# Windows 4 and 5 in 64-token chunks, and one written list for the steady part of a fused attention and MLP kernel

## The chip, the cores and the metric

The kernel runs on one core of a Trainium2 chip. The metric is the device time of one execution in microseconds, as the median of several runs; the profile is one execution that the hardware profiler recorded. PE is TensorE (PEld its weight loads), DVE is VectorE, ACT is ScalarE, POOL is GpSimd, SP is SyncE, which here issues DMAs.

## What is computed

A linear attention with a decay per head, and an MLP behind it with a residual. The reference, cut:

```python
# q, k, v: batch 4, heads 8, tokens 768, head size 64; lam: one decay per head; block = 64
for b in range(nb):
    intra = einsum('bhic,bhjc->bhij', qb, kb) * Dmask        # lam ** (i - j) below the diagonal
    intra = einsum('bhij,bhjd->bhid', intra, vb)
    inter = einsum('bhid,bhde->bhie', qb * lam_pow, kv_state)
    out[:, :, sl] = intra + inter
    kv_state = lam_block * kv_state + einsum('bhsd,bhse->bhde', kb * rev_pow, vb)
# x = out as (4, 768, 512); w_ch1 is 512 x 2048, w_ch2 is 2048 x 512
xn = (x - mu) / sqrt(var + 1e-06) * g_ln
result = x + maximum(xn @ w_ch1, 0) @ w_ch2
```

The length of a chunk is free: with longer chunks the product inside a chunk grows and the states are fewer.

## The kernel before

The work is cut into 12 windows of 256 tokens, u = 0 to 11; window u is of batch u % 4 and holds two pairs (ab = 0, 1) of 64-token blocks. Windows up to 5 (LB = 6) work in chunks of 128 tokens, the others in chunks of 64. A window goes through these steps:

- load_in (L93) issues the DMAs of k, q and v on SP's queue. fill (L72) takes one DMA per tensor for u < LB, whose rows hold two tokens (512 bytes), and two DMAs in rows of one token (256 bytes) otherwise.
- in_k_one, in_q_one and in_v (L229, L233, L239) cast to bf16 and multiply by the decays, mostly on POOL; transpose_dma (L254) transposes q and k by DMA on SP's queue, for windows up to 2 transpose_pe (L244) does it on TensorE.
- With 128 tokens: kv (L311) makes k'v on TensorE; scores and mask (L266, L285) make the masked scores in two halves of the heads; new_state (L337) adds the old state on VectorE and decays the sum on POOL. av (L427) multiplies the masked scores by v into the PSUM tiles po0 and po1.
- With 64 tokens: kv64, scores64, mask64 (L379, L361, L374) and av64 (L416, 32 matmuls where av has 64). states64 (L393) makes, for each j = 0, 1, a sum over the old state (Smid, L405), a second sum (Stmp, L408), the decayed state on POOL (L410) and a copy on POOL (L413). The sums of j = 1 need the decayed state of j = 0.
- inter (L441) adds q times state; norm (L462) copies x to SBUF on ScalarE with its sum, and centers it on VectorE (xc, L477). to_xT (L494) transposes xc: on TensorE for u = 2, 3, 4 (X_PE), else by DMA. rstd_of (L513) makes the squares and the reciprocal root on ScalarE and VectorE.
- The MLP of a window (mlp, L532) is cut into units: m1 (L539, or m1_tile, L651) of 8 or 16 matmuls and a ReLU on ScalarE; then m2 (L667) for windows up to 3, with finish (L700, L708) on VectorE, or m2w (L644) for the later ones. w_sums (L802) makes sums of w2 on VectorE, and h_sums (L557) sums of the hidden units.

[...] kv(u, "po") writes into po0 and po1, which av of the same window writes again; a new tile waits until all who use the old one are done.

The order is written out by hand. The statement manual_schedule() makes every engine issue its instructions in the order in which the program's statements stand, so that an engine's queue is the list of statements, cut to those of this engine. The steady part (L1041 to L1361) takes the units of the MLP from one plan: units(n) issues the next n of it, and between them stand the steps of the windows. For windows 3, 4 and 5 the step is s12(u) (L886: kv, scores, masks, states), then two to four units, then s3(u) (L899: av, inter), one unit or two, and s4(u) (L909). Window 5's last part and window 6 share X1 and X2 (L938, L945); from window 7 on X(u) (L953) holds the second half of window u-1 and the first half of window u.

## Time and profile before

| what | value |
|---|---|
| median of 3 runs | 208.19 us |
| lowest, highest | 207.92, 208.30 us |
| span of the profiled execution, first to last instruction | 205.7 us |
| PE, DVE, ACT, POOL busy | 195.9, 133.4, 122.0, 83.9 us |
| matmuls, and DMA packets under 512 bytes | 3223, 65121 |

For the profiled execution its span is what is told; the runs' times are whole executions, with what lies ahead of the first and behind the last instruction. A row of a timeline gives the start in us from the span's beginning, the length in us, the engine, the line, the operation, out<-in with sizes, how many instructions were merged, and in brackets the idle time before it with what ended it. In the chain of waits a row is a start, a length, the engine, tile and line, and the number of instructions. In the groups, busy us and the mean ns of one stand behind the first bar.

### The profile page before, as it was taken

The page shows a single profiled execution, that of the slowest core. Times are in us where ns is not written, and L with a number is a line of the kernel's source. Part 1 is how long each engine was busy: PE and PEld are TensorE (multiplying, and loading weights), DVE is VectorE, ACT ScalarE, POOL GpSimd, SP SyncE. Part 2 cuts the span into 40 slices and gives each one's busy share as a digit, 9 for nine tenths or more (in the row PEclk, how much of TensorE's full clock was granted, in tenths as well). Part 3 has the DMA queues.
Part 4 walks back from the last instruction along what each step waited for, and adds up shares of the span by engine and source line. Part 5 has one row for each costly group of instructions (what it writes and reads, how often), then busy time and mean ns, then how long its engine had stood idle before and what let it go on. Part 6 is the DMA issues. An engine that isn't in the chain of part 4 may idle for free.

```text
span 205.7 us, 7488 instructions
## 1 busy us (share of the span) xinstructions
PE 195.9 (95%) x3223; PEld 157.8 (77%) x3223; DVE 133.4 (65%) x277; ACT 122.0 (59%) x281; POOL 83.9 (41%) x117
## 2 busy tenths in 40 slices
PE   1997999999999999999999999999999999999992
PEld 0485798545784686489889888888888888988881
DVE  3588352626766458777889774857877947865253
ACT  3787678535357468166575775585586565652630
POOL 5557039317656341464273261772273202002020
PEclk9999999999999999999999999999999999999999
DMA  3999999999899998999799999887988020178404
GB/s 105 301 255 203 179 281 192 198 293 277 194 268 252 217 183 190 170 256 213 165 201 134 220 213 135 207 169 128 234 133 183 4 51 3 26 131 273 139 7 97
DMA packets 91011, 36.41 MB, mean 177 GB/s; under 512 B 65121, under 2 KB 88161, under 8 KB 90978
## 3 DMA queue, kind: packets, MB, share of 16 engines
q1 hardware_dynamic: 86368, 31.53, 74.9%
q0 software_dynamic: 4224, 4.19, 12.7%
q8 instruction: 25, 0.41, 0.9%
q10 hardware_dynamic: 386, 0.20, 0.4%
q14 instruction: 8, 0.07, 0.1%
HBM read 27.27 MB, written 6.29 MB: 163 GB/s over the span
## 4 chain that ended last, share of the span: by engine, by line
PE 85%; DMA 6%; DVE 2%; ACT 2%; SPq 1%; issue 1%; POOL 0%; POOLq 0%; DVEq 0%
PE pm L547 34%; PE pm L684 14%; PE pm1t L658 6%; PE pwd L582 6%; PE pwa L582 6%; PE pwc L582 6%; DMA w<-in_moe_w_ch_dram 4%; PE pwb L582 3%; DMA qin<-in_q_dram 3%; PE po L449 2%; PE po L436 2%; DVE x L595 1%; PE po L423 1%; PE sc L370 1%; PE sc L279 1%; PE pk L324 1%
## 5 line engine op out<-in xcount | busy, mean ns | idle before, releaser
L547 PE MATMUL pm<-xT,w 128*128 128x256 bf16 x640 | 73.9, 273 | 0.4 <-DMA w<-in_moe_w_ch_dram 0.4
L547 PEld LDWEIGHTS <-w 128*128 128x128 bf16 x640 | 61.2, 98 | 8.7 <-DMA w<-in_moe_w_ch_dram 0.5
L550 ACT ACTIVATE hT<-pm 128x512 f16<-128x512 f32 x80 | 47.1, 597 | 28.7 <-PE pm L547 28.5
L684 PE MATMUL pm<-w,hT 128*128 128x512 f16 x128 | 29.8, 380 | 0.0
L582 PEld LDWEIGHTS <-hs 128*128 128x128 f16 x256 | 24.9, 98 | 2.9
L607 POOL TENSOR_TENSOR x<-ev_u,x 128x256 f32<-128x256 f32 x8 | 5.9, 743 | 48.8 <-ACT ev_u L606 37.4
L330 POOL TENSOR_TENSOR Sn<-Stmp,lam_s 128x256 bf16<-128x256 f32 x16 | 9.8, 616 | 33.0 <-DVE Stmp L408 17.9
L565 DVE TENSOR_TENSOR hs<-hT 128x1024 f16<-128x1024 f16 x16 | 12.7, 795 | 15.8 <-ACT hT L550 14.5
L684 PEld LDWEIGHTS <-hT 128*128 128x128 f16 x128 | 11.8, 98 | 12.4
L582 PEld LDWEIGHTS <-hT 128*128 128x128 f16 x192 | 18.7, 98 | 2.1
L658 PE MATMUL pm1t<-xT,w 128*128 128x128 bf16 x256 | 15.6, 219 | 1.0 <-DMA w<-in_moe_w_ch_dram 0.7
L477 DVE SCALAR_TENSOR_TENSOR xc<-po,nmean,g_row 128x512 bf16<-128x512 f32 x18 | 13.0, 745 | 5.0 <-ACT nmean L476 4.9
L658 PEld LDWEIGHTS <-w 128*128 128x128 bf16 x256 | 14.8, 98 | 1.5 <-DMA w<-in_moe_w_ch_dram 0.8
L475 ACT ACTIVATE x<-po 128x512 f32<-128x512 f32 x18 | 10.6, 590 | 7.8 <-PE po L449 4.5
L242 POOL TENSOR_TENSOR vb<-vin,lam_v 128x1024 bf16<-128x1024 f32 (+1 forms) x7 | 11.6, 1659 | 4.8 <-DMA vin<-in_v_dram 4.7
L520 ACT ACTIVATE sq<-x,nmean 128x512 bf16<-128x512 f32 x18 | 12.9, 719 | 0.3
L242 POOL TENSOR_TENSOR vb<-vin,lam_p 128x1024 bf16<-128x1024 f32 x6 | 11.4, 1896 | 3.1 <-ACT hT L550 1.9
L289 DVE TENSOR_TENSOR mA<-sc,keep 128x512 bf16<-128x512 f32 x14 | 9.0, 682 | 4.9 <-PE sc L279 4.9
L661 ACT ACTIVATE hT<-pm1t 128x512 f16<-128x512 f32 x16 | 9.6, 598 | 4.4 <-PE pm1t L658 4.3
L595 DVE SCALAR_TENSOR_TENSOR x<-pwd,rstd,x 128x256 f32<-128x256 f32 x16 | 7.7, 481 | 3.4 <-POOL x L615 3.4
L595 DVE SCALAR_TENSOR_TENSOR x<-pwa,rstd,x 128x512 f32<-128x512 f32 (+1 forms) x16 | 9.1, 612 | 0.8
L582 PE MATMUL pwa<-w,hT 128*128 128x256 f16 x64 | 9.6, 273 | 0.0
(137 smaller groups left out, 318.0 us busy)
## 6 DMA issues: line engine op xcount, KB each, us to landing
out_dram<-x SPq DMA_DIRECT2D x22, 256.0 KB, 4.0
w<-in_moe_w_ch_dram POOLq DMA_DIRECT2D x8, 512.0 KB, 8.0
kin<-in_k_dram SPq DMA_DIRECT2D x14, 256.0 KB, 5.2
qin<-in_q_dram SPq DMA_DIRECT2D x14, 256.0 KB, 4.2
vin<-in_v_dram SPq DMA_DIRECT2D x14, 256.0 KB, 5.3
kin<-in_k_dram SPq DMA_DIRECT2D x5, 512.0 KB, 6.2
qin<-in_q_dram SPq DMA_DIRECT2D x5, 512.0 KB, 7.0
vin<-in_v_dram SPq DMA_DIRECT2D x5, 512.0 KB, 6.1
```

What stands on the lines that cost most here:

```text
L242: eng.tensor_tensor(st[u]["vb"][:, hs], qkv_in[u]["v"][:, hs], lv.to_broadcast([128, n, 2, D]), op=ALU.mult)
L330: eng.tensor_tensor(dst, src, lam_s[:, :, None].to_broadcast([128, NP, D]), op=ALU.mult)
L475: nc.scalar.activation(x, po, ACT.Copy, accum_out=sm)
L477: nc.vector.scalar_tensor_tensor(xc, in0=po, scalar=nm, in1=g_row, op0=ALU.add, op1=ALU.mult)
L520: nc.scalar.activation(sq, s["x"][:, ab], ACT.Square, bias=s["nmean"][:, ab:ab + 1], accum_out=ss[:, ab:ab + 1])
L547: nc.tensor.matmul(pm[:, b, :], lhsT=w1[n // W2K][:, kk, (n % W2K) * 128:(n % W2K + 1) * 128], rhs=xT_of[g][:, kk, 0:N], start=(b == 0 and ...
L550: nc.scalar.activation(hT[:, u * NB:(u + 1) * NB, 0:N], pm, ACT.Relu)
L565: nc.vector.tensor_tensor(s13, b[:, :, 1:2, :].to_broadcast([128, n, 2, 128]), b[:, :, 0:4:3, :], op=ALU.subtract)
L582: nc.tensor.matmul(pr[bank], lhsT=lhs(r), rhs=rhs, start=(first and r == 0), stop=(r == KB // 2 - 1), skip_group_check=True)
L595: nc.vector.scalar_tensor_tensor(out, in0=in0, scalar=r[ab], in1=in1, op0=ALU.mult, op1=ALU.add)
L658: nc.tensor.matmul(pm[:, b, :], lhsT=w1[c][:, kk, b * 128:(b + 1) * 128], rhs=xT_of[g][:, kk, i * 128:(i + 1) * 128], start=(b == 0 and kk ...
L684: nc.tensor.matmul(acc[i], lhsT=hT[:, kk, i * 128:(i + 1) * 128], rhs=w2[kk // W2K][:, kk % W2K, :], start=(kk == 0), stop=(kk == KB - 1))
```

## The change

LB goes from 6 to 4, so windows 4 and 5 are loaded, scaled and multiplied in the form with 64 tokens. kv64 gets a tag for its PSUM tiles. states64 is cut into sums64 (VectorE) and pools64 (POOL), norm's centering becomes center, the squares leave rstd_of as squares, and wind_up of the last window is cut into wind_up and wind_down. Steps such as s12, s3, X are gone: the steady part is one list of single statements, in which each unit of the MLP is named (m1g[g](n), m2s[g](i, part), m2s[g].w(n)). The units keep their order except for a few of windows 0 and 1, for m1g[7](7) and m2s[7].w(0), which change places, and for the first of window 11, which goes ahead of three units. Most steps stand between the same units as before. The core of the diff:

```diff
-    LB = 6
+    LB = 4
...
-    def kv64(u):
+    def kv64(u, tag="mm"):
...
-        s["pk"] = [mm_tile([128, 2, NP, D], F32, f"pk{ab}") for ab in range(2)]
+        s["pk"] = [ps.tile([128, 2, NP, D], F32, tag=f"po{ab}" if tag == "po" else tag, bufs=dict(mm=4, sc=2, po=1)[tag],
+                           name=f"pk{ab}") for ab in range(2)]
...
-    def states64(u, j):
+    def sums64(u, j):
...
+    def pools64(u, j):
...
+    def center(u, ab):
+        s = st[u]
+        po = s["po"][ab].rearrange("p h d -> p (h d)")
+        nc.vector.scalar_tensor_tensor(s["xc"][:, ab], in0=po, scalar=s["nmean"][:, ab:ab + 1], in1=g_row,
+                                       op0=ALU.add, op1=ALU.mult)
...
-    transpose_pe(2, 0, (0, 1, 2, 3), nc.vector)
-    units(1)
-    transpose_pe(2, 1, (0, 1, 2, 3))
+    transpose_pe(2, 1, (0, 1, 2, 3))
     transpose_pe(2, 0, (0, 1, 2, 3), nc.vector)
+    m1b(4)
...
     load_in(3, "k", nc.sync)
+    load_in(3, "v", nc.sync)
     load_in(3, "q", nc.sync)
...
     in_q_one(4, nc.gpsimd, 0)
     in_q_one(4, nc.gpsimd, 1)
-    transpose_dma(4, 0)
     transpose_dma(4, 1)
     load_in(5, "v", nc.sync)
+    in_k_one(4, nc.gpsimd, 1)
...
+    m1g[2](0)
+    transpose_dma(4, 0)
+    m1g[2](1)
+    w_sums(0, 1)
+    m1g[2](2)
+    m1g[2](3)
+    scores(3, 0, early=True)
+    kv(3, "po")
+    new_state(3, 0, nc.gpsimd)
+    scores(3, 1)
+    mask(3, 0)
+    w_sums(1, 0)
     in_v(4, nc.gpsimd)
+    mask(3, 1)
+    new_state(3, 1, nc.gpsimd)
+    m1g[2](4)
+    m1g[2](5)
+    m1g[2](6)
...
+    m1g[2](7)
+    av(3, range(NP))
+    inter(3, 0, fence=False)
+    reader(3)
+    norm(3, 0)
+    m2s[2](0, 0)
+    inter(3, 1)
+    norm(3, 1)
+    center(3, 1)
...
+    m2s[2](0, 3)
+    m2s[2](1, 0)
     transpose_dma(5, 0)
+    center(3, 0)
     to_xT(3, 0)
     to_xT(3, 1)
...
-    units(2)
-    s12(4)
+    m2s[2](1, 1)
+    m2s[2](1, 2)
+    kv64(4, "po")
+    scores64(4)
+    sums64(4, 0)
+    pools64(4, 0)
+    mask64(4, 0)
+    sums64(4, 1)
+    pools64(4, 1)
+    mask64(4, 1)
+    av64(4)
     open_window(6)
+    open_window(7)
     in_k_one(6, nc.scalar, 0)
-    in_k_one(6, nc.gpsimd, 1)
-    units(2)
-    open_window(7)
-    units(2)
-    s3(4)
-    units(1)
+    m2s[2](1, 3)
+    m1g[3](0)
+    m1g[3](1)
+    m1g[3](2)
+    inter(4, 0, fence=False)
+    reader(4)
+    m1g[3](3)
...
-    s12(5)
+    m2s[3](0, 0)
+    m2s[3](0, 1)
+    m2s[3](0, 2)
+    kv64(5, "po")
+    scores64(5)
+    sums64(5, 0)
+    pools64(5, 0)
+    mask64(5, 0)
+    sums64(5, 1)
+    pools64(5, 1)
+    mask64(5, 1)
+    av64(5)
     transpose_dma(6, 1)
-    units(1)
+    m2s[3](0, 3)
```

## The prediction

> **What bounds the kernel now.** I began with the busy time by engine and by stage, because it says whether any engine has idle time that a better order could use.

> ```profile
> 79.00:92.00 13.00, 13.00 (x293) 8.29 (x292) 10.12 (x24) 6.36 (x17) 5.11 (x8) 1.00 1.17 198
> ...
> sum 205.70, PE 195.90 PEld 157.84 DVE 133.44 ACT 122.04 POOL 83.86; mean PE 9.79 PEld 7.89 DVE 6.67 ACT 6.10 POOL 4.19
> ```

> The columns after the stretch are its length and then the busy time of PE, PEld, DVE, ACT and POOL, the granted clock, the DMA share and GB/s. In the 13 us in which windows 5 and 6 are worked on, PE is busy for all 13.00. Over the whole span it is busy for 195.90 of 205.70 us, and what is missing lies in the first 21 us and after the last MLP units. So in the part that the change rewrites TensorE is the bound, without holes. Two things follow: an edit there can gain only as much matmul time as it takes away, and every microsecond for which an edit makes TensorE wait is added to the end in full, since no later hole takes it up.

> Next I read the chain of waits around window 4, because it gives TensorE's order and the real length of each piece.

> ```profile
> 68.88 0.38 PE pk L324 x32
> 69.25 0.23 PE sce L279 x16
> 69.48 0.22 PE sc L279 x16
> 69.70 0.97 PE pm L684 x4
> 70.67 2.62 PE pm L547 x24
> 73.29 0.64 PE po L436 x64
> ```

> This is exactly the order in which the statements stand: kv(4), both halves of the scores, four units of the MLP, then av(4). The four units (0.97 + 2.62 = 3.59 us) are the cover under which VectorE masks the scores and sums the states. TensorE takes its instructions as they are listed, and av(4) does not wait, since its masks are finished when the units are.

> **The change, part by part.**

> *Matmuls of windows 4 and 5.* The form with 64 tokens is run already for windows 6 to 11, so its pieces have rows.

> ```profile
> 88.00 0.29 PE pk L389 x32
> ...
> 101.42 0.37 PE po L423 x32
> ...
> 102.43 0.28 PE sc L370 x32
> ```

> Before, a window takes 0.38 + 0.23 + 0.22 + 0.64 = 1.47 us for these products; in the new form it takes 0.29 + 0.28 + 0.37 = 0.94. If nothing waited, that would be 0.53 us less for each window, 1.06 for both. inter keeps its matmuls.

> *Where av64 now stands.* The new list has kv64(4), scores64(4), the sums, the state products on POOL and the masks, and then av64(4), with m2s[2](1, 3) only behind it; for window 5 it is the same, with m2s[3](0, 3) behind. Between the scores and av64 TensorE has nothing of the MLP. av64 multiplies by the masked scores, and it writes the PSUM tiles po0 and po1, in which kv64(u, "po") has just left the sums that VectorE still reads. So it waits for VectorE's whole chain. Window 7 shows that chain in the same order (sums of j=0, mask, sums of j=1), and window 6 shows how soon it starts after the products:

> ```profile
> 102.47 0.42 DVE L405 TENSOR_TENSOR Smid<-pk,Sn 128x256 f32<-128x256 f32 x1
> 103.00 0.43 DVE L408 TENSOR_TENSOR Stmp<-pk,Smid 128x256 f32<-128x256 f32 x1
> 103.35 0.68 DVE L376 TENSOR_TENSOR mA<-sc,keep 128x512 bf16<-128x512 f32 x1
> 104.16 0.42 DVE L405 TENSOR_TENSOR Smid<-pk,Sn 128x256 f32<-128x256 f32 x1
> 104.61 0.42 DVE L408 TENSOR_TENSOR Stmp<-pk,Smid 128x256 f32<-128x256 f32 x1
> ```
> ```profile
> 88.37 0.42 DVE L405 TENSOR_TENSOR Smid<-pk,Sn 128x256 f32<-128x256 f32 x1 [0.36 <-PE pk L389]
> ```

> The products of window 6 end at 88.00 + 0.29 = 88.29 and the first sum starts at 88.37, 0.08 later. From the first sum to the end of the last one it is 104.61 + 0.42 - 102.47 = 2.56 us, and the second mask behind it takes 0.68 more, 3.24, or a little less where two instructions overlap; I take 3.2. Only the first four matmuls of av64 (pair 0, even head) can go ahead of the second mask. From the start of kv64 to the end of av64 it is 0.29 + 0.08 + 3.2 + 0.37 = 3.94 us in which TensorE does nothing else, where 1.47 us of matmuls stood before: 2.47 us more for a window, 4.9 for both. The scores run inside the wait, and behind the waiting av64 the whole MLP is queued. From below, 2.3 us a window: the first sums could start when the first half of the products is there, about half of 0.29 earlier. From above, 3.0: VectorE may still be at the weight sums or at q of window 6 when window 5's products end, or its instructions may be slowed.

> *center(3, 0).* It moves from behind norm(3, 0) to a place behind m2s[2](1, 0), right ahead of the transposes that read it. On VectorE that puts it behind the reciprocal of rstd_of(3) and the last step of m2s[2](0, 3).

> ```profile
> 64.14 0.75 DVE L477 SCALAR_TENSOR_TENSOR xc<-po,nmean,g_row 128x512 bf16<-128x512 f32 x1 [0.58 <-ACT nmean L476]
> 64.81 0.41 DVE L811 TENSOR_TENSOR wt<-w,wt 128x512 f16<-128x512 f16 x1
> 65.26 0.42 DVE L812 TENSOR_TENSOR wt<-wt,w 128x512 f16<-128x512 f16 x1
> 66.02 0.17 DVE L525 RECIPROCAL rstd<-std 128x2 f32<-128x2 f32 x1 [0.34 <-ACT std L521]
> 66.10 0.73 DVE L708 SCALAR_TENSOR_TENSOR x<-pm,rstd,x 128x512 f32<-128x512 f32 x1
> ```
> ```profile
> 66.70 0.45 PE xt L510 x8
> ```

> The last step (L708) ends at 66.83 and a centering takes 0.75, so xc is there at 67.58, where TensorE comes to the transposes at 66.70: 0.9 us of waiting. Nothing hides it, since the units around it stand where they stood. The lower end is 0.

> *The sums of w2 inside window 3.* w_sums(1, 0) moves from ahead of the window's products to a place between its masks, and new_state(3, 1), whose reading of po1 av(3) waits for, comes behind it.

> ```profile
> 60.12 0.41 DVE L334 TENSOR_TENSOR Stmp<-pk,Sn 128x256 f32<-128x256 f32 x1
> ```
> ```profile
> 61.17 0.64 PE po L436 x64
> ```

> That sum ends at 60.53, so av(3) at 61.17 has 0.64 us in hand; two more weight sums (0.41 + 0.42, as in the rows above) use 0.83. I take 0.2 us of waiting, between 0 and 0.9 (in case they run at half speed beside POOL).

> *The transposes of window 2.* q's transposes now stand ahead of k's, and one half of q comes from POOL:

> ```profile
> 30.79 1.55 POOL L236 TENSOR_TENSOR kq<-qin,lam_q 128x512 bf16<-128x512 f32 x1 [0.34 <-DMA qin<-in_q_dram]
> ```
> ```profile
> 32.19 0.45 PE tp L250 x8
> ```

> POOL ends at 32.34 and TensorE comes at 32.19: 0.2 us, between 0 and 0.3.

> *Loads and queues.* With LB = 4 the loads of windows 4 and 5 run as twelve DMAs of 256 KB in rows of 256 bytes where six of 512 KB in rows of 512 bytes stood, and k of window 4 is transposed behind q and behind the loads of v of window 5, on SP's queue; q of window 3 is loaded behind its v.

> ```profile
> kin<-in_k_dram SPq DMA_DIRECT2D x14, 256.0 KB, 5.2
> ...
> kin<-in_k_dram SPq DMA_DIRECT2D x5, 512.0 KB, 6.2
> ```
> ```profile
> 55.53 5.16 SPq L257 DMA_TRANSPOSE kqT<-kq  x2
> ```
> ```profile
> DMA to landing us min/median/max: 3.3/4.4/7.7
> ```

> Two halves that land 5.2 us after their issue cost between nothing more than one 6.2 us load (they overlap) and 2 x 5.2 - 6.2 = 4.2 us more (one after the other). I take nothing on the path: the transposes of window 4 are all issued by 55.53 + 5.16 = 60.69, and the scores that read them came at 69.25, 8.6 us later, against a median of 4.4 to landing. That cover is thinner in the new order; what it costs when gone is a rival below. POOL gets two state copies more per window and in_v(3), in_v(4) later; the next that need POOL are the states of window 4, after all of that by the same rows. [...]

> *The rest of the list* (squares, readers, masks in another order, stores, wind_down in two, m1g[11](0) two units earlier) changes the order on engines that wait for TensorE, or swaps TensorE's work with TensorE's work: nothing, give or take 0.3 us. The work behind the last units is the same.

> **The sum.** 4.9 + 0.9 + 0.2 + 0.2 = 6.2 us. The profiled span of 205.7 us becomes 211.9. The median of the runs is 208.19 (207.92 to 208.3), 2.5 us above that span for what lies around it; I leave that as it is: 208.2 + 6.2 = **214.4 us**.

> **The rivals.**

> *The wait isn't there* (the other side). If TensorE reached av64 with the masks done, only the smaller products would be left: 208.2 - 1.06 = 207.1 us, faster. It decides from the point at which the 3.2 us chain is covered: some 3 us of units would have to run between scores64 and av64, so that order on TensorE would have to differ from the list. For it: nothing in the profile. Against it: the chain of waits shows the listed order around kv(4) and av(4) to the unit. 4 in 100. This is also the case in which the change doesn't do what it says.

> *The transposes of window 4 come late.* If the added pieces and the new place on SP's queue delay k's transposes by 4.2 us and the landing is the slow one (7.7), they land at 60.69 + 4.2 + 7.7 = 72.6, where scores64(4) would come at about 69.2 + 1.3 = 70.5 (the small waits ahead of it). Up to 2 us more: 214.4 to 216.4. For it: DMA share 1.17 in the stage, a full queue. Against it: medians. 16 in 100.

> *The clock falls in the waits.* TensorE's matmuls were slow at the start of the span:

> ```profile
> 6.55 0.63 PE L752 MATMUL idle<-keep_h,ident 128*128 128x512 bf16 x1
> ```
> ```profile
> L684 PE MATMUL pm<-w,hT 128*128 128x512 f16 x128 | 29.8, 380 | 0.0
> ```

> A matmul over 512 columns takes 0.63 us there and 0.38 later. If a 3 us hole brings the slow rate back for as long as the hole was, 3 us of MLP would take 6, and each window would lose up to 3 us, some 1.5 if it lasts half as long: 214.4 + 3.0 = 217.4 us, with 220.4 as its end. Against it: no hole in this trace behind the start is near 3 us, so nothing tells it; four matmuls also break the hole up. 15 in 100. [...]

> **How the numbers follow.** The forecast as summed has 62 in 100, the late transposes 16, the clock 15, the missing wait 4, and 3 go to waits that I overlooked or that fall away together. With both windows at 2.3 and no small terms it would be 208.2 + 4.6 = 212.8, and 0.4 less if the rest of the list gains; with both at 3.0 and the upper ends of the small waits, 208.2 + 6.0 + 0.9 + 0.9 + 0.3 = 216.3, and the likelier part of the clock rival ends at 217.4. So the range is 212.4 to 217.4. A measurement of this kernel tells about 0.2% (0.4 us) from no change; only the missing wait gets to that: faster 0.03, same 0.02, slower 0.95.

> **What would show it.** In the changed profile TensorE should stand idle ahead of av64 (the L423 group of before) for about 2.5 us and again some tenths, twice, released by VectorE's sums and masks, over 5 us in all; ahead of the transposes of xc of window 3 for about 0.9, released by the centering; PE's busy time should be about 1 us lower and the span near 212. I am wrong if units of the MLP run between scores64 and av64, if the idle time ahead of av64 is under 2 us a window, or if the granted clock falls below 1.00 behind window 4.

## The result

The kernel after takes 220.62 us (median of four executions, 218.21 to 221.24); the kernel before took 208.06 us beside it (207.34 to 208.30). The ratio is 1.0594, 95% interval 1.0532 to 1.0655: 12.6 us slower. The forecast was 214.4, its range ended at 217.4. The direction is right, the size is half. A ratio, here and below, is taken over the executions within 1.5% of the fastest of each kernel, so that it can lie below that of the medians given beside it.

The profiled execution of after is the one of 218.21 us, with a span of 216.5 us. First the page, its times of each engine and the clock in 40 slices of 5.4 us:

```profile
span 216.5 us, 7378 instructions
PE 199.1 (92%) x3159; PEld 158.0 (73%) x3159; DVE 135.9 (63%) x277; ACT 122.3 (56%) x281; POOL 85.9 (40%) x121
PE   2998999999978599599999999999999999999992
PEclk9999999999999999879999999999999999999999
```

Two things differ from the page of before. PE has holes in slices 12, 13, 14 and 17 (digits 7, 8, 5 and 5), where the kernel before has nines. And the clock has an 8 and a 7 in slices 17 and 18: it fell. PE is busy for 199.1 us with fewer matmuls than before, where it was 195.9: part of it ran at a lower clock. The forecast had it 1 us lower; even in e1 below, with the clock kept, it is 196.7.

What TensorE waited for, behind the start (time in all, times, longest, in us):

```profile
PE po L430 <- DVE Smid L405: 3.9, 2, 1.9
PE po L443 <- DVE Stmp L333: 1.5, 1, 1.5
PE xt L522 <- DVE xc L499: 0.8, 1, 0.8
PE po L430 <- DVE mA L375: 0.8, 2, 0.4
...
PE po L430 <- DVE Stmp L410: 0.5, 2, 0.2
```

L430 is av64, L443 is av(3), L522 the transposes of x. The five lines are 7.5 us in all, and each is one that the change made. Their places in the timeline of TensorE (start, length, in brackets the wait ahead and its releaser):

```profile
62.67 0.70 PE L443 MATMUL po<-vb,mA 64*64 64x64 bf16 x63 [1.46 <-DVE Stmp L333]
...
69.12 0.62 PE L522 MATMUL xt<-ident,xc 128*128 128x128 bf16 x8 [0.84 <-DVE xc L499]
...
71.39 0.45 PE L389 MATMUL pk<-vb,kq 64*64 64x64 bf16 x32
71.67 0.47 PE L369 MATMUL sc<-kqT 64*64 64x64 bf16 x32
74.08 0.21 PE L430 MATMUL po<-vb,mA 64*64 64x64 bf16 x1 [1.95 <-DVE Smid L405]
74.54 0.22 PE L430 MATMUL po<-vb,mA 64*64 64x64 bf16 x3 [0.24 <-DVE Stmp L410]
75.14 0.41 PE L430 MATMUL po<-vb,mA 64*64 64x64 bf16 x28 [0.38 <-DVE mA L375]
...
87.22 0.45 PE L389 MATMUL pk<-vb,kq 64*64 64x64 bf16 x32
...
89.88 0.21 PE L430 MATMUL po<-vb,mA 64*64 64x64 bf16 x1 [1.92 <-DVE Smid L405]
...
91.46 5.84 PE L699 MATMUL pm<-w,hT 128*128 128x512 f16 x20
97.37 0.46 PE L389 MATMUL pk<-vb,kq 64*64 64x64 bf16 x32
```

At window 4 TensorE goes from the scores to av64 and stands 1.95, 0.24 and 0.38 us: 2.57 us with four matmuls in between. Window 5 is the same, but behind it twenty matmuls of 128x512 take 5.84 us. In the kernel before such a group took 4.49 us (82.73 to 87.22 in its timeline). The clock by stretches shows why (columns: stretch, its length, busy time of PE, PEld, DVE, ACT and POOL, granted clock, DMA share, GB/s):

```profile
88.00:91.00 3.00, 0.49 (x8) 0.28 (x12) 2.61 (x6) 0.00 (x0) 1.59 (x4) 0.97 0.88 166
91.00:94.00 3.00, 3.00 (x35) 1.29 (x36) 0.62 (x1) 0.00 (x0) 2.32 (x3) 0.50 1.02 212
94.00:97.00 3.00, 3.00 (x15) 1.32 (x13) 0.21 (x2) 0.00 (x0) 0.00 (x0) 0.96 1.01 191
```

The clock stood at one half for all of the middle stretch and for 0.03 x 3 / 0.5 = 0.18 us and 0.04 x 3 / 0.5 = 0.24 us of its neighbours: one fall of 3.4 us, begun at the end of the wait. One such stretch takes 0.5 x 3.4 / 216.5 = 0.008 off the mean clock, which is 0.992 in this execution. In the other three, which have no profile, it is 0.984, 0.983 and 0.984, which fits two stretches, and they took 220.12 to 221.24 us.

Window 4's wait was as long as window 5's, and the clock stayed up behind it. The traces show what differs. Behind the first 19 us and up to the last matmul every half-speed stretch lasts 3.413 us or twice that, and within a trace they begin a whole number of 3.413 us apart (six between 71.52 and 92.00 us in e13 below, five between 74.61 and 91.67 us in e8). Counted back from the fall at 90.81 us in steps of 3.413 us, window 4's wait lies across two steps, the first two rows, and window 5's in one, the third:

```profile
70.32:73.74 3.42, 1.81 (x70) 0.92 (x68) 1.58 (x4) 0.60 (x2) 0.79 (x2) 1.00 1.03 245
73.74:77.15 3.41, 2.45 (x44) 1.64 (x45) 1.90 (x4) 0.32 (x1) 1.12 (x3) 1.00 1.24 219
87.39:90.81 3.42, 1.00 (x68) 0.67 (x59) 2.82 (x6) 0.32 (x2) 1.40 (x3) 1.00 0.72 137
```

TensorE is busy for 1.00 us of the step ahead of the fall, and for 1.81 and 2.45 us of the other two. Counted in this way over all 18 traces, from the first step at full clock to the last matmul, each of the twelve steps with at most 1.49 us of busy time was followed by half speed, of the nine with 1.54 to 1.77 us six were, and no fall began behind one with 1.81 us or more.

Where the time arose is read from the start of the first product of each window (kv) in both traces. In the kernel before the windows 3, 4, 5, 6, 7 and 8 begin at 56.67, 68.81, 81.90, 87.81, 101.75 and 116.69 us.

| from the start of | to the start of | after minus before, us |
|---|---|---|
| the span | window 3 | +0.10 |
| window 3 | window 4 | +2.49 |
| window 4 | window 5 | +2.73 |
| window 5 | window 6 | +4.24 |
| window 6 | window 7 | -0.02 |
| window 7 | the end | +1.22 |

The sum is 10.76 us, the difference of the spans (216.50 - 205.74).

### The profile page after: what moved, and what is told of

Its sections match the earlier page's. It is cut to its first block, busy times and chain, and to the rows that moved or that the text cites. A ratio compares the mean times of both kernels' runs of the same rounds, so it can differ in the third digit from the quotient of the medians.

```text
span 216.5 us, 7378 instructions
## 1 busy us (share of the span) xinstructions
PE 199.1 (92%) x3159; PEld 158.0 (73%) x3159; DVE 135.9 (63%) x277; ACT 122.3 (56%) x281; POOL 85.9 (40%) x121
## 3 DMA queue, kind: packets, MB, share of 16 engines
q0 software_dynamic: 4224, 4.19, 12.1%
## 4 chain that ended last, share of the span: by engine, by line
PE 79%; DVE 7%; DMA 5%; ACT 4%; issue 1%; POOL 1%; POOLq 0%; DVEq 0%
PE pm L562 31%; PE pm L699 12%; PE pm1t L673 6%; PE pwa L597 6%; PE pwd L597 6%; PE pwc L597 6%; DMA w<-in_moe_w_ch_dram 3%; PE pwb L597 3%; DMA lam_b<-in_lam_dram 2%; PE po L456 2%; PE po L430 2%; PE tp L249 1%; PE pk L389 1%; DVE x L610 1%; PE po L443 1%
## 5 line engine op out<-in xcount | busy, mean ns | idle before, releaser
L699 PE MATMUL pm<-w,hT 128*128 128x512 f16 x128 | 30.9, 392 | 0.0
L699 PEld LDWEIGHTS <-hT 128*128 128x128 f16 x128 | 12.2, 100 | 13.9 <-issue 1.8
L580 DVE TENSOR_TENSOR hs<-hT 128x1024 f16<-128x1024 f16 x16 | 12.4, 772 | 15.1 <-ACT hT L565 13.9
L241 POOL TENSOR_TENSOR vb<-vin,lam_p 128x1024 bf16<-128x1024 f32 x8 | 15.7, 1964 | 7.8 <-DMA vin<-in_v_dram 7.8
L235 POOL TENSOR_TENSOR kq<-qin,lam_p 128x512 bf16<-128x512 f32 x13 | 13.5, 1056 | 2.2 <-DMA qin<-in_q_dram 2.2
L405 DVE TENSOR_TENSOR Smid<-pk,Sn 128x256 f32<-128x256 f32 x16 | 6.8, 423 | 6.7 <-PE pk L389 4.5
L723 DVE SCALAR_TENSOR_TENSOR x<-pm,rstd,x 128x512 f32<-128x512 f32 x8 | 5.9, 742 | 7.8 <-PE pm L699 7.8
L375 DVE TENSOR_TENSOR mA<-sc,keep 128x512 bf16<-128x512 f32 x16 | 10.7, 680 | 0.0
L467 ACT COPY seen<-po 128x8 f32<-128x8 f32 x12 | 1.4, 169 | 16.2 <-PE po L456 16.2
## 6 DMA issues: line engine op xcount, KB each, us to landing
out_dram<-x SPq DMA_DIRECT2D x22, 256.0 KB, 3.6
kin<-in_k_dram SPq DMA_DIRECT2D x18, 256.0 KB, 4.9
qin<-in_q_dram SPq DMA_DIRECT2D x18, 256.0 KB, 5.2
vin<-in_v_dram SPq DMA_DIRECT2D x18, 256.0 KB, 5.4
w<-in_moe_w_ch_dram POOLq DMA_DIRECT2D x8, 512.0 KB, 7.6
kin<-in_k_dram SPq DMA_DIRECT2D x3, 512.0 KB, 6.1
qin<-in_q_dram SPq DMA_DIRECT2D x3, 512.0 KB, 7.0
vin<-in_v_dram SPq DMA_DIRECT2D x3, 512.0 KB, 8.1
```

The source lines that it names most:

```text
L235: eng.tensor_tensor(part(1, st[u]["kq"], ALL)[:, :, :, j], src[:, :, :, j], lq[:, :, :, None].to_broadcast([128, NP, 2, D]), op=ALU.mult)
L241: eng.tensor_tensor(st[u]["vb"][:, hs], qkv_in[u]["v"][:, hs], lv.to_broadcast([128, n, 2, D]), op=ALU.mult)
L375: nc.vector.tensor_tensor(s["mA"][:, e], s["sc"][e], keep64[:, None, None, :].to_broadcast([128, NP, 2, D]), op=ALU.mult)
L580: nc.vector.tensor_tensor(s13, b[:, :, 1:2, :].to_broadcast([128, n, 2, 128]), b[:, :, 0:4:3, :], op=ALU.subtract)
L699: nc.tensor.matmul(acc[i], lhsT=hT[:, kk, i * 128:(i + 1) * 128], rhs=w2[kk // W2K][:, kk % W2K, :], start=(kk == 0), stop=(kk == KB - 1))
```

## The experiments

The theory: the two waits ahead of av64 cost what was forecast; what was missing is a fall of the clock in most of them, a weight sum on VectorE that GpSimd held up, and about 1 us behind window 6. The rivals: the 64-token chunks with their smaller loads cost it, or the new order behind window 6. The labels are numbered in the order in which they ran; "the repaired list" is the new list with four places put back.

**e1_av_late: the products back behind units of the MLP.**

```diff
-    av64(4)
     open_window(6)
...
+    av64(4)
     inter(4, 0, fence=False)
```

and the same for window 5.

> The changed kernel with av64(4) and av64(5) moved down to just ahead of inter(4, 0) and inter(5, 0), so that four units of the MLP run between the masks' start and av64. Theory (the waits ahead of av64 cost themselves, and the clock falls because of them): TensorE's idle time ahead of av64 goes from 5.2 us to under 0.3, the granted clock stays at 1.00, and the time goes from 220.6 to 210 to 211.5 us. Rival (the clock falls for another reason, such as a late transfer, or the added time lies in the transfers): the clock still falls behind window 4 or 5, and the time stays at 213 us or more.

Measured: 214.99 us, ratio 1.0318 (1.0260 to 1.0376). 5.6 us came back, and the clock is 1.000 in the profiled execution; the waits at L430 are gone. In the other three executions the mean clock is 0.992, 0.992 and 0.984, so in them it still fell, at places that no profile shows. But the time is 4 us short of what was expected, because TensorE now waits elsewhere:

```profile
105.55 0.45 PE L369 MATMUL sc<-kqT 64*64 64x64 bf16 x32 [2.28 <-DMA kqT<-kq]
...
147.90 0.61 PE L597 MATMUL pwc<-wt,hs 128*128 128x256 f16 x4 [1.44 <-DVE hs L580]
```

The scores of window 7 wait 2.28 us for a transpose by DMA, and a product of window 7 waits 1.44 us for a sum on VectorE. Neither wait is in the list of after, whose own waits came earlier and covered them. Windows 4 and 5 now take 0.42 us less each than in the kernel before (the offset falls from 1.69 to 1.27 to 0.85), which is the gain that the change could have had there. It is not steady: in e4 below, with the same products in the same places, they take 0.07 and 0.36 us more.

**e2_fill: the clock kept up in the waits.** Nothing is taken away; TensorE gets work of no use in each wait.

```diff
+    unread_mm(8)
     av64(4)
```

and the same for window 5: eight matmuls of 128x512 into a PSUM tile that nobody reads.

> The changed kernel with av64 where it is, and ahead of each av64 eight more matmuls of 512 columns whose result nobody reads (about 1.7 us of work inside a wait of some 2 us). Theory: the waits end at the same instants, since VectorE's chain sets them, but the granted clock stays at 1.00, so that of the 220.6 us only the loss by the clock goes, two falls of 3.4 us at half rate, 3.4 us: 216.8 to 217.6 us. Rival (the fall costs nothing that the wait hasn't taken already, or falls for another reason): 219.5 us or more.

Measured: 219.19 us, ratio 1.0515 (1.0450 to 1.0580); the clock did not fall in either wait:

```profile
87.00:92.00 5.00, 4.13 (x109) 2.15 (x108) 3.45 (x7) 1.09 (x3) 2.20 (x5) 1.00 0.61 115
92.00:97.00 5.00, 5.00 (x72) 2.49 (x70) 1.63 (x4) 0.55 (x3) 1.70 (x2) 1.00 1.15 224
```

Window 4 cost 2.73 us over the kernel before and window 5 2.72, where after had 2.73 and 4.24. So the fall is worth 1.5 us and the wait 2.7. The total missed: 2.26 us arose between windows 9 and 10 for 0.87 in after, 1.4 more, where a sum on VectorE came late (below, with e9). The price of a fall rests on the traces: the intervals of e2 and after overlap.

**e3_pool: the weight sum without GpSimd beside it.** in_v(4) on GpSimd moves from beside w_sums(1, 0) to behind the state of window 3.

```diff
     w_sums(1, 0)
-    in_v(4, nc.gpsimd)
...
     new_state(3, 1, nc.gpsimd)
+    in_v(4, nc.gpsimd)
```

> The changed kernel with in_v(4) on POOL moved behind new_state(3, 1), so that no POOL instruction runs beside the weight sums of w_sums(1, 0); these stay between the masks of window 3. Theory (the first weight sum took 1.9 us because POOL worked beside it): its length falls to about 0.42 us and the wait ahead of av(3) from 1.46 us to 0 to 0.3. Rival (the order alone is to blame, or VectorE waits for data): the weight sum stays above 1.2 us or the wait above 0.8 us.

The first weight sum in after stands beside GpSimd's product for v; VectorE and GpSimd there:

```profile
58.84 1.91 DVE L823 TENSOR_TENSOR wt<-w 128x512 f16<-128x512 f16 x1
60.68 0.41 DVE L824 TENSOR_TENSOR wt<-w 128x512 f16<-128x512 f16 x1
```
```profile
58.58 1.90 POOL L241 TENSOR_TENSOR vb<-vin,lam_p 128x1024 bf16<-128x1024 f32 x1 [1.56 <-DMA vin<-in_v_dram]
```

And in e3:

```profile
60.98 0.41 DVE L823 TENSOR_TENSOR wt<-w 128x512 f16<-128x512 f16 x1
...
67.01 1.19 DVE L826 TENSOR_TENSOR wt<-w,wt 128x512 f16<-128x512 f16 x1
68.24 1.15 DVE L827 TENSOR_TENSOR wt<-wt,w 128x512 f16<-128x512 f16 x1
...
70.03 0.73 DVE L499 SCALAR_TENSOR_TENSOR xc<-po,nmean,g_row 128x512 bf16<-128x512 f32 x1
```

The sum takes 0.41 us instead of 1.91, and the wait ahead of av(3) is gone from the list. The time is not better (221.22 us in one execution, with three half-speed stretches, one of them from 21.5 us on, far ahead of the edit). Of the 1.46 us only 0.4 are saved between windows 3 and 4 (2.05 us over the kernel before, for 2.49), since the other two weight sums now run beside GpSimd's products for q (1.19 and 1.15 instead of 0.42 and 0.43 us), and the centering behind them makes the transposes wait 1.91 us instead of 0.84. That the weight sums are long beside GpSimd's products is shown on both sides; the saving is not.

**e4_all, e5_order, e11_rep_st: four places put back, then the queue of SyncE.** e4 has e1's edit and, as in the kernel before, center(3, 0) behind norm(3, 0), w_sums(1, 0) ahead of scores(3, 0), the transposes of window 2, and m1g[7](7) ahead of m2s[7].w(0).

> The changed kernel with av64 of windows 4 and 5 ahead of inter, center(3, 0) behind norm(3, 0), w_sums(1, 0) ahead of window 3's products, k's transposes of window 2 first again and m1g[7](7) ahead of m2s[7].w(0). Theory (these five places are the whole loss, and the smaller products of windows 4 and 5 are a gain of 1.06 us): no wait of TensorE above 0.4 us behind the first 21 us, clock 1.00, 206.6 to 207.6 us, below the 208.06 of before. Rival (the loads in rows of 256 bytes or the rest of the list cost something that these waits hid): 208.2 us or more.

Measured: 214.72 us, ratio 1.0283 (1.0212 to 1.0354), a miss. From window 3 to window 7 the offset to the kernel before stays between 2.56 and 2.99 us (2.50 of it stand at window 2 already, from a load of weights at the start for which TensorE waited 1.9 us and a fall of the clock in that wait), so the repairs hold; then 4.4 us arise between windows 7 and 8, where the scores wait 2.06 us for a transpose and the clock falls in that wait (0.9 us of it is one MLP unit that the new list has ahead of window 8, and is given back by window 9). On SyncE the two transposes of window 7 (L256) stand apart, between stores (L731) and a transpose of x (L515):

```profile
94.54 1.61 SPq L731 DMA_DIRECT2D out_dram<-x  x2
96.31 2.10 SPq L256 DMA_TRANSPOSE kqT<-kq  x1
98.47 1.36 SPq L731 DMA_DIRECT2D out_dram<-x  x2
99.93 2.36 SPq L515 DMA_TRANSPOSE xT<-xc  x1
102.82 1.55 SPq L256 DMA_TRANSPOSE kqT<-kq  x1
```

e5 puts the transposes ahead of the stores, e11 the stores behind the loads of window 8:

```diff
-    store(1)
     transpose_dma(7, 0)
-    store(2)
-    to_xT(5, 0)
     transpose_dma(7, 1)
+    to_xT(5, 0)
+    store(1)
+    store(2)
```

> The four repairs of e4 (late attention products of windows 4 and 5, centre, weight sum and transposes of windows 3 and 2 as before, the last unit of the first matmul of pair 7 ahead) and beside them SyncE's queue as in the kernel before: both transposes of window 7 ahead of the two stores, v of window 7 loaded ahead of k of window 8. The theory after e4: the waits ahead of the attention products hid a second fault, the transpose of q of window 7 behind a store and a transpose of x; it landed 2.1 us too late and the clock fell in that wait (1.5 us). By it the wait at the scores of window 7 goes and the time is 214.7 less 2.1 to 3.6 and less what follows from it: 208.0 to 211.5, with windows 3 to 8 within 1 us of the kernel before. Rival: SyncE is late as a whole (twelve more loads of 64-token halves, a microsecond each), so the transposes only change places with the stores and the wait stays or moves to window 8: 213 to 215.

> The repaired list of e4 in chunks of 64 tokens, the transposes of x of window 5 and of q and k of window 7 back in the order of the kernel before, and the two stores behind the loads of window 8. In e5 the stores stood ahead of the second transpose of x of window 5, and the matmuls of pair 5 waited 2.0 us for it. If a queue of transfers that is 3 to 5 us late is what holds the repaired list at 215, this ends it: 207.6 to 209.5. If something else of the list's order costs (VectorE behind the load of q of window 6, ScalarE behind its k), 211 to 215.

Measured: e5 215.16 us, ratio 1.0337 (1.0308 to 1.0366), and e11 215.28 us, 1.0306 (1.0235 to 1.0376). Both missed. In e5 the wait changed its place, to the next transpose in the queue:

```profile
107.86 5.25 PE L562 MATMUL pm<-xT,w 128*128 128x256 bf16 x32 [2.01 <-DMA xT<-xc]
```

TensorE also waits 1.5 us for a sum on VectorE (L580). This fits the rival, that the queue is late as a whole and not by the order of a few transfers. In e11 the waits are again at transposes of q and k (1.14 us at window 4, 0.77 at window 5, 2.0 further on).

**e6_old64, e10_old64_st, e12_old64_mask: the chunks without the list.** In e6 the kernel before has the 64-token form for pairs 4 and 5 and no other change:

```diff
-    LB = 6
+    LB = 4
...
-    s12(4)
+    s12_64(4)
...
-        av(u, range(NP))
+        if u < LB:
+            av(u, range(NP))
+        else:
+            av64(u)
```

with s12_64 as kv64, scores64 and then states64 and mask64 for each half, and the same for window 5.

> The kernel before with nothing changed but the chunks: pairs 4 and 5 loaded and computed in chunks of 64 tokens, each step where the kernel before has it, its attention products where the 128-token products were. It separates the chunks from the list. Theory that the list alone is at fault: two sets of smaller products save 0.53 us each, the two more 64-token state steps of each window lie on VectorE and GpSimd beside matmuls, and the time is 207.0 to 208.3. Rival, that the loads of 64-token halves and the longer chain of state steps cost something by themselves (SyncE about 4 us later by window 7, the transposes of window 7 with a margin of 2.8 us in the kernel before): 209.5 to 213, with a wait at the scores of window 5, 6 or 7 for a transpose.

Measured: ratio 1.0074 (1.0046 to 1.0103), median 210.36 us. By themselves the chunks cost some 1.5 us by the ratio; the seven executions reach from 208.94 to 214.86 us. The profiled execution took 214.86, above the median, so that its profile shows the weak place and not the usual loss: the transposes of window 7 are issued from 99.42 on instead of 93.88 in the kernel before, and the scores wait:

```profile
105.77 0.45 PE L370 MATMUL sc<-kqT 64*64 64x64 bf16 x32 [2.89 <-DMA kqT<-kq]
```

The matmuls saved are few: kv and scores of window 5 take 0.70 us from start to the next unit where they took 0.83, the products 0.48 where they took 0.53.

e10 moves the stores of windows 1 and 2 behind the loads of window 8, e12 also has both masks ahead of the state sums.

> The kernel before with only its chunks changed, and the stores of windows 1 and 2 (four transfers of 256 KB, some 3.7 us of issues on SyncE) moved from ahead of the transposes of window 7 to behind the loads of window 8. If late transfers are all that the chunks cost there, the wait of 2.9 us and the fall of the clock at the scores of window 7 go, what is left is 0.45 us at window 4 (its second mask), and the time is 207.6 to 208.6, with a narrow spread. Rival, the transfers are short as a whole and the lateness passes on to k, q and v of window 8 or to the transposes of x: 209.5 to 213.

> As e10, and in windows 4 and 5 both masks ahead of the state sums on VectorE, since the attention products wait for the masks and only the later products for the states. In e6 the products of window 4 waited 0.38 us for the second mask. With it gone the smaller products are left as a gain, 0.13 to 0.2 us in each window (scores and products of window 5: 0.70 and 0.48 against 0.83 and 0.53 us): 207.0 to 208.1, at or a little below the kernel before. Rival, the states then come late for the products with them and the wait only changes its name: as e10.

Measured: e10 211.57 us, 1.0155 (1.0107 to 1.0202); e12 211.49 us, 1.0177 (1.0140 to 1.0215). Both missed, and neither beats the kernel before. In e10 the scores wait for a transpose 0.3 us in all, but the lateness passes on: 1.0 us at a transpose of x and 0.9 us that the profile gives no releaser for. In e12 the wait for the mask became one for the states, as its rival said:

```profile
74.55 0.19 PE L450 MATMUL po<-Sm,kqT 64*64 64x64 bf16 x1 [0.56 <-POOL Sm L414]
...
89.15 0.19 PE L450 MATMUL po<-Sm,kqT 64*64 64x64 bf16 x1 [0.56 <-POOL Sm L414]
```

**e7_new128, e9_rep128: the list without the chunks.** e7 is after with LB = 6 and the 128-token forms in the same places, av(4) where av64(4) stood; e9 the same with e4's list.

> The kernel after with nothing changed but the chunks: pairs 4 and 5 in chunks of 128 tokens as before, on the new list, the products of attention right behind the scores and masks. If the list alone is at fault, the wait ahead of the products stays: four masks and two state sums stand on VectorE ahead of it, some 3.3 us beside 1.5 us of scores and products, so 2 to 3 us in each window, a fall of the clock in most of them, and the time is 217 to 222. If the chunks carry the loss (their chain of four state steps, their loads), it falls to 208 to 213.

> The repaired list of e4, with pairs 4 and 5 back in chunks of 128 tokens, so with the loads of 512 KB. Loads and list apart: with 64-token chunks the transposes of windows 4 to 7 land 3 to 6 us later than in the kernel before (66.5 and 67.3 against 63.3 and 64.2 us at window 4, 105.7 against 99.7 at window 7, in the kernel before with only its chunks changed), while the products of windows 3 to 6 stand where they stood. If the 256-KB loads make the transfers late, the wait of 2.1 us at the scores of window 7 and the clock's fall in it go with them: 207.6 to 209.5. Rival, the order of the list makes them late (v of window 5 ahead, the stores between the transposes): the wait stays, 212 to 216.

Measured: e7 222.49 us, ratio 1.0699 (1.0665 to 1.0734): the list alone costs more than list and chunks together. Its first wait at window 4 is not for the masks but for the state sum that reads the PSUM tiles:

```profile
74.23 0.21 PE L443 MATMUL po<-vb,mA 64*64 64x64 bf16 x1 [1.50 <-DVE Stmp L333]
75.75 1.06 PE L443 MATMUL po<-vb,mA 64*64 64x64 bf16 x63 [1.31 <-DVE Stmp L333]
```

e9 gives 211.08 us, 1.0096 (1.0055 to 1.0137), between its two theories. The wait at the scores of window 7 fell from 2.06 us in e4 to 0.26, so it comes with the 64-token chunks. That it is their 256-KB loads, and not their longer chain of state steps, is argued from SyncE's queue (last section). In its profiled execution (214.07 us, above the median) 4.7 us arise between windows 9 and 10, with a fall of the clock, where VectorE's sums (L580, 0.68 us in the kernel before) stand beside GpSimd's product for v:

```profile
142.77 2.38 DVE L580 TENSOR_TENSOR hs<-hT 128x1024 f16<-128x1024 f16 x1
```
```profile
142.25 2.35 POOL L241 TENSOR_TENSOR vb<-vin,lam_p 128x1024 bf16<-128x1024 f32 x1
```

It is the same collision as in window 3. q of window 10 comes late, and the new list has in_v(10) behind GpSimd's half of q, where the kernel before had it ahead; so the product for v falls on the sums. e2 lost its 1.4 us to the same: there VectorE's product for q, 0.74 us in the kernel before, took 2.30 us beside GpSimd's product for v, and the sums came behind it.

**e8_fill2: a smaller dose.** As e2, with 2 unread matmuls instead of 8, in a single execution.

> The kernel after with 2 instead of 8 unread matmuls of 128x512 in each wait ahead of the products of windows 4 and 5 (0.43 us of matmuls in a wait of 2.0 us, so some 1.5 us stay idle in one stretch). A dose for the clock: if it falls only where the idle of a 3.41-us stretch passes some 2 us in sum, two unread matmuls keep it in both windows, and the profile shows 2.7 us lost in each and no fall there; if any stretch of over a microsecond brings it down, one or both windows lose 4.2. One look: the time is 217.5 to 221.

Measured: 219.47 us, clock 0.984, with falls from 74.6 and from 91.7 us in the trace, one behind each wait. With two matmuls (0.43 us) it fell behind both waits, with eight (1.7 us, e2) behind neither.

**e13 to e16: the terms added up while the waits stay.** e13 is the complement of e1: av64 stays, the other four places are put back. e14 adds e2's eight matmuls. e15 and e16 are e13 and e14 with every step from the states of window 6 on in the order of the kernel before.

> The kernel after with its attention products of windows 4 and 5 where it has them, and the other four places put back as in the kernel before: weight sum of window 3 ahead of its scores, centre of (3,0) at once, transposes of window 2, the last unit of the first matmul of pair 7 ahead of the first product of w. The complement of e1. If the profile's terms add up while the two waits stay (weight sum beside GpSimd 1.46, centre 0.84, the swapped product 0.87 us), it is 220.6 - 3.2 = 217.4, 216.6 to 218.2, with windows 4 and 5 at 2.7 us each and a fall of the clock of 1.5 us in one or both. Rival, these terms too only hide one another as those under the waits did: 219 to 221.

> As e13, with 8 unread matmuls of 128x512 in each of the two waits ahead of the products of windows 4 and 5, which in e2 kept the clock up. What is left of the change is then the two waits alone, 2.7 us each, and the stretch of 0.3 us behind window 5: 208.1 + 5.4 + 0.3 = 213.8, 213.3 to 214.8, 3.0 us or so under e13. Rival: the clock's falls are not what e13 loses beyond the two waits, but late transfers or sums further on, and it is within 1 us of e13.

> As e13, and from the states of window 6 on every step in the order of the kernel before. e13 missed by 1.7 us: in its profile one fall lasted two stretches of 3.4 us, and 1.2 us more went between the states of windows 7 and 8. If the new order behind window 6 costs that by itself, this is 1.0 to 2.0 us under e13: 217.2 to 218.2. Rival: what comes behind window 6 follows from the late transfers of the 64-token loads in either order, as in e10 and e12 on the old list (1.5% over the kernel before): 218.6 to 220.

> As e14, and from the states of window 6 on every step in the order of the kernel before. What is left of the change are the two waits and the chunks. e14 lost 4 us behind window 6 in its profile, with sums on VectorE 1.3 us late. If the new order there is the cause: 208.1 + 5.4 + 0.3 = 213.8, 213.3 to 215.3. Rival: the chunks' late transfers cost it in either order, and it is 216 to 219 again.

| kernel | us | ratio and interval |
|---|---|---|
| e13_rest | 219.14 | 1.0540 (1.0499 to 1.0582) |
| e14_rest_fill | 218.27 | 1.0476 (1.0407 to 1.0545) |
| e15_rest_tail | 219.45 | 1.0518 (1.0439 to 1.0597) |
| e16_rest_fill_tail | 214.32 | 1.0318 (1.0274 to 1.0362) |

e16 is as expected, the other three missed. In e13 window 3 costs nothing any more (-0.20 us from its start to that of window 4, for +2.49 in after), but the swapped product gained nothing (0.82 us arise between windows 9 and 10, for 0.87 in after), and behind window 4 the clock fell for two stretches in a row:

```profile
70.00:73.00 3.00, 1.02 (x33) 0.71 (x34) 2.24 (x5) 0.00 (x0) 1.91 (x4) 0.75 1.00 244
73.00:76.00 3.00, 3.00 (x15) 1.53 (x12) 0.75 (x1) 0.62 (x1) 0.00 (x0) 0.50 1.20 230
76.00:80.00 4.00, 4.00 (x41) 2.96 (x40) 0.45 (x3) 1.79 (x3) 0.47 (x1) 0.71 1.03 172
```

That is (0.25 x 3 + 0.50 x 3 + 0.29 x 4) / 0.5 = 6.8 us at half speed. e15 shows the price across executions: 217.04 us at a mean clock of 0.992, 218.75 at 0.984, 220.50 and 220.16 at 0.977, so for one, two and three stretches, some 1.65 us each. By the same measure e13's executions, at 0.972 to 0.984, had no fewer of them, so why e15 is not faster than e13 stays open.

With the clock kept and the old order behind window 6, e16 is what the forecast had summed. TensorE at window 4 in e16:

```profile
68.64 0.45 PE L394 MATMUL pk<-vb,kq 64*64 64x64 bf16 x32
...
69.53 1.67 PE L313 MATMUL unread_mm<-w 128*128 128x512 bf16 x7 [0.16 <-issue]
...
72.39 0.41 PE L435 MATMUL po<-vb,mA 64*64 64x64 bf16 x28 [0.38 <-DVE mA L380]
72.73 0.82 PE L704 MATMUL pm<-w,hT 128*128 128x512 f16 x3
```

One of the eight unread matmuls has no record. The block from kv64 to the next unit is 72.73 - 68.64 = 4.09 us. In the traces windows 4 and 5 cost 2.74 and 2.87 us over the kernel before, 5.6 together, and everything else 1.1. e16 has neither the late weight sum nor the late centering, so that it lands on the forecast to 0.1 us is partly chance; that the waits alone are worth 5.6 us is not. With the new order behind window 6 (e14) the median is 4 us higher, and in its profiled execution, the longest of its four, TensorE waits 2.1 us for VectorE's sums; window 5 cost 3.36 us there, since VectorE was still at the weight sums and at q of window 6 when the products ended. Between e13 and e15, where the clock falls in the waits, the same edit gained nothing. So the order costs time in some versions and not in others. Which of its steps does, beyond the collision of in_v(10) with the sums, was not tried one by one and stays open.

## Why the prediction was wrong

**The two waits: right.** 2.47 us was forecast for a window, 2.73 was measured (2.72 to 2.87 with the clock kept, and 3.36 once, in e14, for the reason that was given for the upper end of 3.0). The block is 4.1 us for the forecast's 3.94, and what it replaced was 0.83 + 0.53 = 1.36 us from start to start, for 1.47. The chain is as drawn: VectorE's sums first, the mask last.

**center(3, 0): right**, 0.84 for 0.9. **The transposes of window 2: nothing** (the start of window 3 is 0.10 later), for 0.2.

**The clock: the step that failed.** The sum had nothing for it. The rival had a chance of 15 in 100, with the reason that no hole was near 3 us and that four matmuls break it up. The hole is 2.57 us in three pieces, and it brought the clock down all the same, in after behind window 5, where 1.00 us of matmuls was left in the step of 3.413 us that held the wait. In the profiles with both waits as in after (after, e3, e13 and e15) the clock fell behind six of eight. That two falls are the usual case in after is read from the mean clocks alone, and a stretch can lie elsewhere: e3, e4 and e14 have one at 21.5 to 23.2 us, behind a wait for weights, and some executions of the kernel before have a mean clock of 0.992. The rival's price was right, 3.0 us for both at 1.5 us a fall. That 3 us would take 6 was the author's estimate; the granted clock in the fall is 0.50, and the 128x512 matmuls there have the length of its slow row, 0.63 us, for 0.38 behind the fall (L699 in after, 635 and 379 ns in the mean). Its 217.4 us is also the end of the range: the range held the fall of the clock or the upper ends of the small waits, and both came. In the 18 traces each step of 3.413 us with up to 1.49 us of matmuls in it was followed by half speed, and so were the two of e8, with 0.43 us of large matmuls more and some 1.6 us in all; with 1.7 us of them the clock stayed (e2).

**The weight sum: mis-sized**, 1.46 us for 0.2, above the upper end of 0.9. The forecast let it run "at half speed beside POOL", as the author's estimate. The rows fit an instruction that stands, not one that runs at half speed: it began 0.26 us behind GpSimd's product, ended 0.27 us behind that one's end (60.75 and 60.48), and took 0.41 us when alone (e3). The kernel before has such a pair too, ahead of window 3:

```profile
53.96 1.18 DVE L811 TENSOR_TENSOR wt<-w,wt 128x512 f16<-128x512 f16 x1
```
```profile
52.81 2.05 POOL L236 TENSOR_TENSOR kq<-qin,lam_q 128x512 bf16<-128x512 f32 x2
```

That sum took 1.18 us, for 0.41 at 64.81 us, and ended 0.28 us behind GpSimd's second product (55.14 and 54.86). By these rows a sum begun early in a product of 1.90 us would take some 1.9 us. The masks, with one input in PSUM, ran beside the product for v in the kernel before (57.51 to 59.41 us) at 1.29 and 1.28 us for two, and at 1.28 with GpSimd idle (59.78 us in e3).

**Loads and queues: "nothing on the path" held in after only because the waits hid it.** With the waits gone a transpose is some 2 us late at window 7 (2.28 in e1, 2.06 in e4; in e5 2.01, for a transpose of x). The chunks alone cost 0.74% on the old list.

**The rest: 1.2 us for 0 give or take 0.3**, all of it behind window 7 in small pieces, the longest 0.3 us. That the list causes it is not shown: with the old order from window 6 on, 1.4 us (e15) and 1.3 us (e16) arise there too.

The sum for the profiled execution of after: 2 x 2.73 + 2.49 (1.46 + 0.84 and 0.2 of other things) + 1.51 for one fall + 1.2 + 0.1 = 10.8 us, as measured. The median of 220.6 fits a second fall. Of the 6.2 us between it and the forecast, two falls are 3.0, the weight sum 1.3, what lies behind window 7 1.2 and the two waits 0.5.

List and chunks apart: the chunks alone 1.0074, the list alone 1.0699, both 1.0594. By these ratios the chunks save some 2 us on the new list and cost 1.5 on the old one; on the repaired list (e4 and e9) they cost some 4. No version tried is faster than the kernel before.

## What to carry to other kernels

In an order written out by hand, look for what stands on the in-order engine between a producer's input and its consumer: the MLP units between scores and products were worth 2.7 us a window, and the units were still there, only behind. Price a wait of TensorE of some 2 us with the clock that it may cost afterwards (1.5 to 1.7 us a fall here), and count the executions, not one profile, for how often it does. And when one wait is repaired and the gain is half of what was expected, look for the next wait that it had hidden before doubting the repair.

## What the runs showed of the hardware

Sums of two fp16 operands on VectorE that began while GpSimd multiplied ended 0.27, 0.28 and 0.55 us behind GpSimd's product: 1.91 for 0.41 us (after), 1.18 for 0.41 (before), 2.38 for 0.68 (e9). Such a step of VectorE beside a GpSimd product cost 1.5 us in after, 0.8 in before and 1.7 in e9.

Twelve loads of 256 KB in pieces of 256 bytes in place of six of 512 KB set the transposes of window 7 back by 5.5 us on SyncE's queue (99.42 for 93.88 in e6's profiled execution, with TensorE 0.5 us behind by then), though a 256-KB load of k took 5.2 us from issue to landing in both, by the median. What grew is their time on the queue: the issues of these loads stand there for 6.5 us in the kernel before and for 13.4 to 15.1 us in after, e4, e6, e10 and e12. Whether it is twice the number of DMAs or the shorter pieces was not tried apart.
